# A Fourier filter and a squared-ReLU FFN in one kernel: the load of W_in, the prologue around it, and the slots of two FFT stages

## The chip, the cores and the metric

The kernel runs on one core of a Trainium2 chip. A core has five engines that work side by side and wait for each other through semaphores: PE (TensorE, matrix products into PSUM), DVE (VectorE), ACT (ScalarE), POOL (GpSimd) and SP (SyncE, which here only issues transfers). Transfers between the chip's main memory and on-chip memory run on 16 DMA engines. The metric is the device time of one execution in microseconds (us), and the median of several runs is compared.

## What is computed

x has 8 batches of 3008 positions and 256 channels. Each batch is filtered along its positions in the frequency domain, and every filtered position then goes through a feed-forward network (FFN) with 2048 hidden units:

```python
X = np.fft.rfft(x, axis=1)
Y = X * (filt_r + 1j * filt_i)[None, :, :]
y = np.fft.irfft(Y, n=3008, axis=1)            # (8, 3008, 256)
h = np.maximum(y.reshape(24064, 256) @ w_in, 0.0)
out = h * h @ w_out                            # (24064, 256)
```

Inputs and output are float32; the products on PE are made in float16 with float32 sums.

## The kernel before

**FFT stages.** 3008 = 64 x 47, so both transforms are matrix products in two steps. Of one batch: stage A multiplies x with a 47-point matrix (result u), u goes through main memory (dU) and comes back in another order as ut; stage B multiplies ut with a 64-point matrix, and DVE multiplies the result with the filter (unit_b: one product of 128 x 1024 values, two copies; unit_s: an addition); stage P is the way back (ze), which goes through main memory (dZ) and returns as zt; stage Y gives y, stored as yt. A batch has 16 units of A, 12 of B and P, 16 of Y.

**FFN.** The 24064 rows are cut into 47 groups of 512. A group takes eight slots. In each slot `ffn_g1` makes four 512-column matmuls with W_in for this group, ACT applies ReLU to the 128 x 1024 result, DVE squares it (`ffn_sq`), and `ffn_g2` makes eight 256-column matmuls with W_out for the group before. The first group (slots 0 to 7) has no group before it.

**Order.** Nothing is reordered: each engine works through its instructions in program order. The loop at L731 emits a slot at a time, and `fft_plan(b)` says into which slot, and at which of two places in it, each FFT unit of batch b goes (`put(slot, place, unit)`). Slots are counted from 40 to 48 before the group in which batch b begins; for batch 1 they are the absolute slots. A unit put into a slot stands on PE between that slot's matmuls, on DVE and ACT between the squares and ReLUs, and its transfers stand in SP's queue.

**Prologue.** All of batch 0's stages up to the first quarter of Y, and three quarters of stage A of batch 1, are made ahead of the FFN loop (L653 to L723). There stage A of batch 0 is `chunk_a0` (its result is turned by `turn_u`); `place_f(im, k)` spreads the filter's real (im = 0) or imaginary part over sF with PE, copied out by an engine that is given; `unit_p0` is stage P; `chunk_a` is stage A of batch 1. x of batches 0 and 1 comes by `load_wide` in three tiles of 1 MB, cast to float16 by `cast_wide`. Before `unit_b` of batch 0 starts, `place_f` has run for (0,0) to (0,3) and (1,0).

**Buffers.** A pool hands out its buffers in turn, and a new tile waits until all readers of the buffer's last tile are done. p_x32 has two buffers of 8 KB per partition: in turn x of batch 0 (two tiles), W_in (two tiles of 1 MB), x of batch 1 (two tiles). p_u has three: two of sSPx (a second copy of stage P's weights, made by POOL), then u of batch 1, chunks 0, 2, 1, 3 in that order. p_y has two: filt_r and filt_i, x of batch 1 (third tile), the products of batch 0, then yt. PSUM is split among psF, psO and psH, two buffers each; all FFT units in the FFN loop use psF.

**Queues.** SP issues nearly all transfers in program order. In the prologue: x of batch 0 (the first two tiles in halves), the filters, constants, W_in, the third tile of x of batch 1; then the writes of dZ, between which the other two tiles of x of batch 1 stand (L709); then two reads of zt, half of W_out, two reads of zt, the other half, and three writes of dU.

Of the kernel before, what the change touches and what calls it, by code (L numbers as in the profile page):

```python
# [9 lines left out]
F16 = mybir.dt.float16  # L10
F32 = mybir.dt.float32
# [7 lines left out]
N1, N2, NC, NM = 64, 47, 24, 32  # L19
# [91 lines left out]
def kernel(  # L111
# [96 lines left out]
    sPF = p_out.tile([128, 6, 128], F16, tag="ost", name="sPF")  # L208

    xw32, xw16 = {}, {}  # L210
    halves, later = ((0, 0), (0, 1)), []

    def load_wide(b, k):

        v0 = xrows[b * S:b * S + 2048, :].rearrange("(p m) d -> p m d", m=16)
        v1 = xrows[b * S + 2048:b * S + 3072, :].rearrange("(p m) d -> p m d", m=8)
        pool, tag = (p_x32, "x32") if k < 2 else (p_y, "yt") if b else (p_h2, "h2")
        t = pool.tile([128, 8, D], F32, tag=tag, name=f"xw_{b}_{k}")
        v = (v0[:, 0:8, :], v1, v0[:, 8:16, :])[k]
        for m in (slice(0, 4), slice(4, 8)) if (b, k) in halves else (slice(0, 8),):  # L220
            if m.stop > 4 and m.start == 4:
                later.append((t, v, m))
            else:
                nc.sync.dma_start(out=t[:, m, :], in_=v[:, m, :])
        xw32[(b, k)] = t

    def cast_wide(b, k, *engs, parts=(0, 1)):
        if 0 in parts:
            xw16[(b, k)] = p_x16.tile([128, 8, D], F16, tag="x16", name=f"xw16_{b}_{k}")
        for i in parts:  # L230
            m = slice(4 * i, 4 * i + 4)
            engs[i].tensor_copy(out=xw16[(b, k)][:, m, :], in_=xw32[(b, k)][:, m, :])

    for k in range(2):
        load_wide(0, k)
    for t, v, m in later:
        nc.sync.dma_start(out=t[:, m, :], in_=v[:, m, :])
    load_wide(0, 2)


    f32s = []
# [33 lines left out]

    f16s = []

    def place_f(im, k, eng, rotate=False):

        if rotate:  # L280
            banks, groups = bank_pair(f"psf_{im}_{k}")
        else:
            t = psH(f"psf_{im}_{k}")
            banks, groups = [t[:, 0, :], t[:, 1, :]], [(t, 0)]
        for i in range(4):
            c = 4 * k + i
            e0, e1 = D * c, D * (47 - c)
            cuts = [0] + [d for d in range(1, D)
                          if (e0 + d) % QF == 0 or (c and (e1 + d) % QF == 0)] + [D]
            for d0, d1 in zip(cuts, cuts[1:]):  # L290
                o = banks[i // 2][:, (i % 2) * D + d0:(i % 2) * D + d1]
                q, a = divmod(e0 + d0, QF)
                nc.tensor.matmul(o, sPF[:, PQ.index((0, q)), :], f16s[0][:, im, a:a + d1 - d0],  # L293
                                 start=True, stop=False)
                q, a = divmod(e1 + d0, QF) if c else (0, QF + d0)
                nc.tensor.matmul(o, sPF[:, PQ.index((1, q)), :], f16s[0][:, im, a:a + d1 - d0],  # L296
                                 start=False, stop=True)
        for t, i in groups:
            n = t.shape[1]
            dst = sF[:, im, 4 * k + 2 * i:4 * k + 2 * i + 2 * n, :]  # L300
            src = t.rearrange("p t (a d) -> p (t a) d", d=D)
            if eng is nc.scalar:
                eng.activation(out=dst, in_=src, func=AF.Copy, scale=sign[:, 0:1] if im else 1.0)  # L303
            elif im:
                eng.tensor_scalar_mul(out=dst, in0=src, scalar1=sign[:, 0:1])
            else:
                eng.tensor_copy(out=dst, in_=src)
# [2 lines left out]
    sWout = const.tile([128, NJT, 256], F16, name="sWout")  # L310
    w32s = {}

    def load_win(k):
        w32s[k] = p_x32.tile([128, DFF], F32, tag="x32", name=f"win32_{k}")
        nc.sync.dma_start(out=w32s[k], in_=moe_w_in[128 * k:128 * k + 128, :])

    def cast_win(k):
        for j in range(2):
            c = slice(1024 * j, 1024 * j + 1024)
            nc.gpsimd.tensor_copy(out=sWin[:, k, c], in_=w32s[k][:, c])  # L320

    def load_wout(k):
        if k == 0:
# [22 lines left out]
    def unit_a(b, a):  # L346

        c, i = divmod(a, 4)
        if i == 0:
            us[(b, c)] = p_u.tile([96, 8, D], F16, tag="u", name=f"u_{b}_{c}")  # L350
        ps = psF(f"psA_{b}_{a}")
        m = slice(2 * i, 2 * i + 2)
        if b == 1:
            nc.tensor.matmul(ps[0:96, :], s1[:, c // 2, :], xw16[(b, 2 * (c % 2))][:, m, :],
                             start=True, stop=False)
            nc.tensor.matmul(ps[0:96, :], s1[0:120, 2 + c, :], xw16[(b, 1)][0:120, m, :],
                             start=False, stop=True)
        else:
            nc.tensor.matmul(ps[0:96, :], sSA, x16s[(b, c)][:, m, :], start=True, stop=True)  # L359
        o = us[(b, c)][:, 2 * i:2 * i + 2, :]  # L360
        pv = ps[0:96, :].rearrange("p (a d) -> p a d", d=D)
        if a % 2 == 0:
            nc.scalar.copy(out=o, in_=pv)  # L363
        else:
            nc.vector.tensor_copy(out=o, in_=pv)  # L365
        if i == 3:
            write_u(b, c)
# [21 lines left out]
                else:  # L389
                    eng.tensor_copy(out=o, in_=pv)  # L390

    def chunk_a0(c, ks):

        for k in ks:
            banks, groups = bank_pair(f"psA_0_{c}_{k}")
            for dt in range(2):
                for i in range(4):
# [210 lines left out]
    def fft_plan(b):  # L608
# [3 lines left out]
        def put(r, place, f, *a):  # L612
            plan.setdefault((r, place), []).append((f, a))

        if b == 1:
            for n in range(4, 16):
                put(n if n < 8 else n + 2 if n < 12 else 2 * n - 7, n % 2, unit_y, 0, n)
            for k in range(4):
                put((4, 5, 7, 7)[k], 1, cast_wout, k, nc.vector)
        t0 = 2 if b == 1 else 6  # L620
        for a in range(12 if b == 1 else 0, 16):
            put(t0 + a // 2, a % 2, unit_a, b, a)
        put(10 if b == 1 else 14, 1, read_u, b)
        t0 = 14 if b == 1 else 18
        for p in range(12):
            r = t0 + (18 if b == 1 else 19) * p // 11
            put(r, 0, unit_b, b, p)
            put(r, 0, unit_s, b, p)
            put(r + 2, 1, unit_p, b, p)
        t0 = 35 if b == 1 else 40  # L630
        for c in range(4):
            put(t0, 1, read_z, b, c)
        if b + 1 < B:
# [5 lines left out]
                if c < 2:  # L639
                    put(r, 1, load_x, b + 1, c + 2)  # L640
        for n in range(16):
            if b == 1:
                put(38 + n // 2 if n > 3 else 39, n % 2, unit_y, b, n)
            else:
                put(44 + n // 2, n % 2, unit_y, b, n)
        return plan

    def run(plan, r, place):
# [2 lines left out]


    uT = p_h2.tile([128, 2, NC, 128], F16, tag="h2", name="uT")  # L653
    for i in range(2):
        for k in range(2):
            cast_wide(0, k, nc.vector, nc.vector, parts=(i,))
    cast_wide(0, 2, nc.vector, nc.gpsimd)

    def load_const(t, d, k):
        c = slice(12 * k, 12 * k + 12)  # L660
# [2 lines left out]
    for k in range(2):  # L663
        c = slice(12 * k, 12 * k + 12)
        load_const(sSB[:, c, :], dSB, k)
        load_const(sSP[:, c, :], dSP, k)
    for k in range(2):
        load_win(k)
    for k in range(2):
        for c in (0, 2):  # L670
            chunk_a0(c, (k,))
    for k in range(2):
        for c in (1, 3):
            chunk_a0(c, (k,))
    f16s.append(p_h2.tile([128, 2, QF + D], F16, tag="h2", name="f16"))
    e0, e1 = slice(0, 1504), slice(1504, QF)
    for im in range(2):
        nc.gpsimd.tensor_copy(out=f16s[0][:, im, QF:], in_=nyq[:, im, :])
    for im, e in ((0, e0), (0, e1), (1, e0)):
        nc.gpsimd.tensor_copy(out=f16s[0][:, im, e], in_=f32s[im][:, e])  # L680
    for k in range(2):
        sSPx.append(p_u.tile([128, 12, 128], F16, tag="u", name=f"sSPx_{k}"))
        c = slice(12 * k, 12 * k + 12)
        nc.gpsimd.tensor_copy(out=sSPx[k][0:64], in_=sSP[64:128, c, :])
        nc.gpsimd.tensor_copy(out=sSPx[k][64:128], in_=sSP[0:64, c, :])
    for k in range(2):
        cast_win(k)
    uts[0] = p_ut.tile([128, NC, D], F16, tag="ut", name="ut_0")
    load_wide(1, 2)
    cast_wide(1, 2, nc.gpsimd, nc.gpsimd)  # L690
    for k in range(6):
        turn_u(k, nc.vector if k in (1, 3, 4, 5) else nc.scalar)
        if k > 2:
            place_f(0, k - 3, nc.scalar, True)
    nc.vector.tensor_copy(out=f16s[0][:, 1, e1], in_=f32s[1][:, e1])
    place_f(0, 3, nc.vector, True)
    place_f(1, 0, nc.scalar)
    for k in range(7):
        if k < 6:
            unit_b(0, 2 * k)  # L700
            if k < 5:
                place_f(1, k + 1, nc.scalar)
            unit_b(0, 2 * k + 1)
        if k > 0:
            unit_p0(k - 1)
        if k < 2:
            place_f(0, k + 4, nc.scalar)
        if k in (1, 2):
            load_wide(1, k - 1)  # L709
            cast_wide(1, k - 1, nc.gpsimd, nc.gpsimd)  # L710
    read_z(0, 0)
    load_wout(0)
    read_z(0, 1)
# [59 lines left out]
```

## Time and profile before

| | |
|---|---|
| median of 7 runs | 795.35 us (794.32 to 798.26) |
| the profiled execution | 798.78 us, of which the span from the first to the last instruction is 797.0 us |
| mean clock granted to PE | 0.995 |
| first FFN matmul (psH, L560) | starts at 52.71 us |
| first W_out matmul (psO, L577; slot 8) | starts at 63.87 us |
| DMA engines | 46.6% of the span busy with SP's queue |

Times in the profile count from the start of the span. In the chain of work each line is a start, a duration, and the engine and line that ran or the transfer that was waited for. In the table of stretches the columns are: length, busy time of PE, of PE's weight loads, of DVE, ACT and POOL (with the number of instructions), granted PE clock as a share of full, busy share of the DMA engines, and GB/s. In the table of waits: who waited, for whom, us in total, number of times, the longest. In SP's timeline: start, us, line, and what is issued, with the number of transfers in a merged row.

### The profile page before, as it was taken

What the parts mean: (1) busy time and instruction counts of PE and PEld (TensorE: products, weight loads), DVE (VectorE), ACT (ScalarE), POOL (GpSimd) and SP (SyncE); (2) the same over time, 40 slices, a digit from 0 to 9 for tenths busy, and PEclk for the clock granted to TensorE, in tenths of its full rate; (3) what the DMA queues carried; (4) which work ended last, traced back from release to release, by engine and by line L of the source; (5) the groups of instructions that cost most, each with busy time, mean ns of one, the idle gap of its engine ahead of it and who ended that gap; (6) DMA issues with size and microseconds to landing.
All of it is one profiled execution on the core that took longest, in us unless ns stands there. A gap on an engine that the chain in (4) does not pass through costs nothing.

```text
span 797.0 us, 14801 instructions
## 1 busy us (share of the span) xinstructions
PE 783.5 (98%) x6102; PEld 553.7 (69%) x6102; DVE 552.3 (69%) x898; ACT 554.9 (70%) x708; POOL 24.7 (3%) x27
## 2 busy tenths in 40 slices
PE   8989999999999999999999999999999999999998
PEld 5846677667676677867778676776767666776666
DVE  6946995579755897559965699557995579554342
ACT  3856777767767677767776677676777767766664
POOL 3710000000000000000000000000000000000000
PEclk9989999999999999999999999999999999999999
DMA  9994555336713468055471555425564342521111
GB/s 353 358 274 138 136 144 140 91 127 166 207 52 107 151 163 188 29 162 152 125 183 49 169 156 134 131 68 158 149 176 95 87 138 80 122 52 41 40 41 53
DMA packets 88139, 107.32 MB, mean 135 GB/s; under 512 B 6288, under 2 KB 78864, under 8 KB 83856
## 3 DMA queue, kind: packets, MB, share of 16 engines
q1 hardware_dynamic: 87864, 106.19, 46.6%
q8 instruction: 48, 0.79, 0.4%
q10 hardware_dynamic: 144, 0.18, 0.1%
q14 instruction: 19, 0.16, 0.1%
q0 software_dynamic: 64, 0.00, 0.0%
HBM read 58.12 MB, written 48.23 MB: 133 GB/s over the span
## 4 chain that ended last, share of the span: by engine, by line
PE 92%; DMA 4%; ACT 1%; DVE 1%; issue 0%; POOL 0%; SPq 0%; ACTq 0%; DVEq 0%; POOLq 0%
PE psO L577 40%; PE psH L560 38%; PE psA L359 3%; PE psY L530 3%; PE psB L443 2%; PE psP L494 2%; DMA ut<-dU 2%; PE warm L274 1%; DMA xw<-in_x_dram 1%; PE psf L293 1%; DMA zt<-dZ 1%; ACT h L564 1%; PE psf L296 1%; DMA dU<-u 0%; PE psA L380 0%; ACT sF L303 0%
## 5 line engine op out<-in xcount | busy, mean ns | idle before, releaser
L564 ACT ACTIVATE h<-psH 128x1024 f16<-128x1024 f32 x376 | 385.2, 1025 | 190.7 <-PE psH L560 189.2
L577 PE MATMUL psO<-sWout,h 128*128 128x256 f16 x3008 | 388.6, 272 | 0.0
L560 PE MATMUL psH<-yt,sWin 128*128 128x512 f16 (+7 forms) x1728 | 386.9, 351 | 1.8 <-DVE yt L539 0.8
L577 PEld LDWEIGHTS <-h 128*128 128x128 f16 x3008 | 290.5, 98 | 77.3
L568 DVE TENSOR_TENSOR h<-h 128x1024 f16<-128x1024 f16 x376 | 253.8, 685 | 100.7 <-ACT h L564 99.2
L560 PEld LDWEIGHTS <-sWin 128*128 128x128 f16 x1728 | 159.5, 98 | 101.7 <-issue 3.5
L451 DVE TENSOR_TENSOR prod<-psB,sF 128x1024 f16<-128x1024 f32 x84 | 102.4, 1219 | 6.9 <-PE psB L443 6.6
L539 DVE CAST yt<-psY 128x376 f16<-128x376 f32 x62 | 33.9, 549 | 57.4 <-PE psY L530 57.4
L365 DVE CAST u<-psA 96x512 f16<-96x512 f32 x50 | 34.3, 687 | 47.3 <-PE psA L359 45.1
L496 ACT CAST ze<-psP 128x512 f16<-128x512 f32 x84 | 49.3, 586 | 17.8 <-PE psP L494 15.9
L588 ACT COPY ost<-psO 128x512 f32<-128x512 f32 (+1 forms) x96 | 55.7, 580 | 6.7 <-PE psO L577 5.3
L530 PEld LDWEIGHTS <-zt 112*128 112x128 f16 x512 | 34.8, 98 | 12.2 <-issue 2.4
L530 PE MATMUL psY<-sC,zt 112*128 112x94 f16 x512 | 42.3, 205 | 0.6 <-DMA zt<-dZ 0.3
L465 DVE TENSOR_TENSOR yf<-prod,yf 128x512 f16<-128x512 f16 x84 | 35.7, 425 | 2.9
L443 PE MATMUL psB<-ut,sSB 128*128 128x256 f16 x192 | 36.5, 272 | 1.2 <-DMA ut<-dU 0.9
L359 PE MATMUL psA<-x,sC 94*96 94x512 f16 x96 | 36.6, 382 | 0.0
L443 PEld LDWEIGHTS <-sSB 128*128 128x128 f16 x192 | 18.6, 98 | 21.9 <-issue 2.8
L494 PE MATMUL psP<-yf,sSP 128*128 128x256 f16 x168 | 32.1, 273 | 0.2 <-ACT yt L537 0.2
L537 ACT CAST yt<-psY 128x376 f16<-128x376 f32 x66 | 30.7, 468 | 1.1 <-PE psY L530 0.6
L338 DVE CAST x<-x 94x2048 f16<-94x2048 f32 x24 | 29.2, 1216 | 0.0
L363 ACT CAST u<-psA 96x512 f16<-96x512 f32 x50 | 28.6, 572 | 0.0
L458 DVE COPY yf<-prod 64x512 f16<-64x512 f16 x84 | 24.3, 289 | 2.9
(63 smaller groups left out, 256.5 us busy)
## 6 DMA issues: line engine op xcount, KB each, us to landing
x<-in_x_dram SPq DMA_DIRECT2D x20, 768.0 KB
zt<-dZ SPq DMA_DIRECT2D x64, 192.0 KB
dU<-u SPq DMA_DIRECT2D x28, 384.0 KB
dZ<-ze SPq DMA_DIRECT2D x28, 384.0 KB
out_dram<-ost SPq DMA_DIRECT2D x66, 128.0 KB
out_dram<-ost SPq DMA_DIRECT2D x31, 256.0 KB
ut<-dU SPq DMA_DIRECT2D x7, 1024.0 KB
xw<-in_x_dram SPq DMA_DIRECT2D x4, 1024.0 KB
```

The source lines that it names most:

```text
L359: nc.tensor.matmul(ps[0:96, :], sSA, x16s[(b, c)][:, m, :], start=True, stop=True)
L443: nc.tensor.matmul(ps[:, i * D:(i + 1) * D], sSB[:, 2 * p + i, :], uts[b][:, 2 * p + i, :], start=True, stop=True)
L451: nc.vector.tensor_mul(out=prod, in0=ps.rearrange("p (a d) -> p a d", d=D).unsqueeze(1).to_broadcast([128, 2, 2, D]), in1=sF[:, :, 2 * p:2 ...
L465: nc.vector.tensor_add(out=yf, in0=prod[:, 0], in1=yf)
L494: nc.tensor.matmul(ps[:, i * D:(i + 1) * D], sSP[:, 2 * p + i, :], yf[:, i, :], start=True, stop=True)
L496: nc.scalar.copy(out=zes[(b, c)][:, 2 * i6:2 * i6 + 2, :], in_=ps.rearrange("p (a d) -> p a d", d=D))
L530: nc.tensor.matmul(ps[:, 94 * jj:94 * jj + 94], zt[:, 4 * (g % 2) + jj, dt * 128:(dt + 1) * 128], sSY, start=True, stop=True)
L560: nc.tensor.matmul(ps[:, i, o:o + n], sWin[:, dt, jt * 128:(jt + 1) * 128], yts[b][:, dt, r:r + n], start=(dt == 0), stop=(dt == 1))
L564: nc.scalar.activation(out=h2[:, 2 * s:2 * s + 2, :], in_=ps, func=AF.Relu)
L568: nc.vector.tensor_mul(out=v, in0=v, in1=v)
L577: nc.tensor.matmul(pso[g][:, t % 2, :], h2s[g][:, jt, t * 128:(t + 1) * 128], sWout[:, jt, :], start=(jt == 0), stop=(jt == NJT - 1))
L588: nc.scalar.copy(out=ost[:, h0:h0 + step, :], in_=pso[g][:, h0:h0 + step, :])
```

## The change

- W_in is loaded in seven pieces of 256 to 768 columns, into buffers of p_ze, p_prod and p_yf that nobody uses yet. All three x tiles of batch 1 are therefore issued right after it, ahead of the writes of dZ. POOL casts the seven pieces.
- x of batch 0 is loaded in whole tiles, and `chunk_a0` goes chunk by chunk.
- In `turn_u`/`place_f`: only (0,0), (0,1) and (1,0) come before `unit_b` of batch 0; (0,2) to (0,5) come between its units, copied by ACT. The cast of filt_i is split over DVE, POOL and ACT. sSPx is made in six pairs of copies instead of two.
- The third x tile of batch 1 is cast by DVE and ACT after `unit_b` and `unit_p0` of batch 0; POOL casts the first two.
- Last quarter of stage A of batch 1: slots 1 to 4 instead of 8 and 9, all four copied by DVE. The Y units 8 to 11 of batch 0 sit in slots 8 to 11 instead of 10 to 13. W_out is cast by POOL in slots 1, 2, 4 and 5, instead of DVE in slots 4, 5, 7 and 7.
- Batch 1: stage B ends one slot earlier (slot 31), the reads of zt, loads and casts of x come one slot earlier, and Y takes two units in each of slots 38 to 45; before, four were in slot 39.
- Batches 2 to 7: stage B starts at offset 19 instead of 18, with the last unit at 37 as before, and Y at 45 instead of 44.

```diff
-    def load_win(k):
-        w32s[k] = p_x32.tile([128, DFF], F32, tag="x32", name=f"win32_{k}")
-        nc.sync.dma_start(out=w32s[k], in_=moe_w_in[128 * k:128 * k + 128, :])
+    def load_win():
+        for k, c, n, pool, tag in ((0, 0, 768, p_ze, "ze"), (0, 768, 768, p_ze, "ze"),
+                                   (0, 1536, 512, p_prod, "prod"), (1, 0, 768, p_ze, "ze"),
+                                   (1, 768, 512, p_prod, "prod"), (1, 1280, 512, p_prod, "prod"),
+                                   (1, 1792, 256, p_yf, "yf")):
+            t = pool.tile([128, n], F32, tag=tag, name=f"win32_{k}_{c}")
+            nc.sync.dma_start(out=t, in_=moe_w_in[128 * k:128 * k + 128, c:c + n])
+            wins.append((t, k, slice(c, c + n)))
...
-        if a % 2 == 0:
+        if a % 2 == 0 and b > 1:
             nc.scalar.copy(out=o, in_=pv)
...
-                put(n if n < 8 else n + 2 if n < 12 else 2 * n - 7, n % 2, unit_y, 0, n)
+                put(n if n < 12 else 2 * n - 7, n % 2, unit_y, 0, n)
             for k in range(4):
-                put((4, 5, 7, 7)[k], 1, cast_wout, k, nc.vector)
-        t0 = 2 if b == 1 else 6
+                put((1, 2, 4, 5)[k], 1, cast_wout, k, nc.gpsimd)
+        t0 = 6
         for a in range(12 if b == 1 else 0, 16):
-            put(t0 + a // 2, a % 2, unit_a, b, a)
+            put(a - 11 if b == 1 else t0 + a // 2, a % 2, unit_a, b, a)
         put(10 if b == 1 else 14, 1, read_u, b)
-        t0 = 14 if b == 1 else 18
+        t0 = 14 if b == 1 else 19
         for p in range(12):
-            r = t0 + (18 if b == 1 else 19) * p // 11
+            r = t0 + (17 if b == 1 else 18) * p // 11
...
-        t0 = 35 if b == 1 else 40
+        t0 = 34 if b == 1 else 40
...
-            if b == 1:
-                put(38 + n // 2 if n > 3 else 39, n % 2, unit_y, b, n)
-            else:
-                put(44 + n // 2, n % 2, unit_y, b, n)
+            put((38 if b == 1 else 45) + n // 2, n % 2, unit_y, b, n)
...
-    for k in range(2):
-        load_win(k)
-    for k in range(2):
-        for c in (0, 2):
-            chunk_a0(c, (k,))
-    for k in range(2):
-        for c in (1, 3):
-            chunk_a0(c, (k,))
+    load_win()
+    for k in range(3):
+        load_wide(1, k)
+    for c in (0, 2, 1, 3):
+        chunk_a0(c)
...
-    for im, e in ((0, e0), (0, e1), (1, e0)):
-        nc.gpsimd.tensor_copy(out=f16s[0][:, im, e], in_=f32s[im][:, e])
+    for e in (e0, e1):
+        nc.gpsimd.tensor_copy(out=f16s[0][:, 0, e], in_=f32s[0][:, e])
+    uts[0] = p_ut.tile([128, NC, D], F16, tag="ut", name="ut_0")
+    turn_u(0, nc.scalar)
+    turn_u(1, nc.vector)
+    turn_u(2, nc.scalar)
+    turn_u(3, nc.vector)
+    place_f(0, 0, nc.scalar, rotate=True)
+    for eng, e in ((nc.vector, slice(0, 1024)), (nc.gpsimd, slice(1024, 2048)),
+                   (nc.scalar, slice(2048, QF))):
+        cast(eng, f16s[0][:, 1, e], f32s[1][:, e])
+    turn_u(4, nc.vector)
+    place_f(0, 1, nc.scalar, rotate=True)
+    turn_u(5, nc.vector)
+    place_f(1, 0, nc.scalar, nc.vector, rotate=True)
...
-    for k in range(2):
-        cast_win(k)
-    uts[0] = p_ut.tile([128, NC, D], F16, tag="ut", name="ut_0")
-    load_wide(1, 2)
-    cast_wide(1, 2, nc.gpsimd, nc.gpsimd)
-    for k in range(6):
-        turn_u(k, nc.vector if k in (1, 3, 4, 5) else nc.scalar)
-        if k > 2:
-            place_f(0, k - 3, nc.scalar, True)
-    nc.vector.tensor_copy(out=f16s[0][:, 1, e1], in_=f32s[1][:, e1])
-    place_f(0, 3, nc.vector, True)
-    place_f(1, 0, nc.scalar)
+    cast_win()
+    for k in range(2):
+        cast_wide(1, k, nc.gpsimd, nc.gpsimd)
...
-        if k < 2:
-            place_f(0, k + 4, nc.scalar)
-        if k in (1, 2):
-            load_wide(1, k - 1)
-            cast_wide(1, k - 1, nc.gpsimd, nc.gpsimd)
+        if k < 4:
+            place_f(0, k + 2, nc.scalar)
+    cast_wide(1, 2, nc.vector, nc.scalar)
```

More of the change, by code (lines that the diff above doesn't have):

```diff
@@ L210 @@
     xw32, xw16 = {}, {}
-    halves, later = ((0, 0), (0, 1)), []
     def load_wide(b, k):
@@ L218, in load_wide, with cast, cast_wide @@
         t = pool.tile([128, 8, D], F32, tag=tag, name=f"xw_{b}_{k}")
[L219 to L222, printed above, removed]
-            else:
-                nc.sync.dma_start(out=t[:, m, :], in_=v[:, m, :])
-        xw32[(b, k)] = t
[L227 to L230, printed above, removed]
+        nc.sync.dma_start(out=t, in_=(v0[:, 0:8, :], v1, v0[:, 8:16, :])[k])
+        xw32[(b, k)] = t
+    def cast(eng, out, in_):
+        (eng.copy if eng is nc.scalar else eng.tensor_copy)(out=out, in_=in_)
+    def cast_wide(b, k, *engs):
+        t = p_x16.tile([128, 8, D], F16, tag="x16", name=f"xw16_{b}_{k}")
+        for i in range(2):
             m = slice(4 * i, 4 * i + 4)
-            engs[i].tensor_copy(out=xw16[(b, k)][:, m, :], in_=xw32[(b, k)][:, m, :])
-    for k in range(2):
+            cast(engs[i], t[:, m, :], xw32[(b, k)][:, m, :])
+        xw16[(b, k)] = t
+    for k in range(3):
         load_wide(0, k)
-    for t, v, m in later:
-        nc.sync.dma_start(out=t[:, m, :], in_=v[:, m, :])
-    load_wide(0, 2)
     f32s = []
@@ L276, with place_f @@
     f16s = []
-    def place_f(im, k, eng, rotate=False):
+    def place_f(im, k, *engs, rotate=False):
         if rotate:
@@ L299, in place_f @@
             n = t.shape[1]
+            eng = engs[i % len(engs)]
             dst = sF[:, im, 4 * k + 2 * i:4 * k + 2 * i + 2 * n, :]
@@ L311, with cast_win @@
     w32s = {}
-    def load_win(k):
-        w32s[k] = p_x32.tile([128, DFF], F32, tag="x32", name=f"win32_{k}")
-        nc.sync.dma_start(out=w32s[k], in_=moe_w_in[128 * k:128 * k + 128, :])
[L317 to L320, printed above, removed]
+    def load_win():
[6 more added lines that the diff above has]
+            wins.append((t, k, slice(c, c + n)))
+    def cast_win():
+        for t, k, c in wins:
+            nc.gpsimd.tensor_copy(out=sWin[:, k, c], in_=t)
+    wins = []
     def load_wout(k):
@@ L390, in chunk_a, with chunk_a0 @@
                     eng.tensor_copy(out=o, in_=pv)
-    def chunk_a0(c, ks):
-        for k in ks:
+    def chunk_a0(c):
+        for k in range(2):
             banks, groups = bank_pair(f"psA_0_{c}_{k}")
@@ L641, in fft_plan @@
         for n in range(16):
-            if b == 1:
-                put(38 + n // 2 if n > 3 else 39, n % 2, unit_y, b, n)
-            else:
-                put(44 + n // 2, n % 2, unit_y, b, n)
+            put((38 if b == 1 else 45) + n // 2, n % 2, unit_y, b, n)
         return plan
@@ L653 @@
     uT = p_h2.tile([128, 2, NC, 128], F16, tag="h2", name="uT")
-    for i in range(2):
-        for k in range(2):
-            cast_wide(0, k, nc.vector, nc.vector, parts=(i,))
-    cast_wide(0, 2, nc.vector, nc.gpsimd)
+    for k in range(3):
+        cast_wide(0, k, nc.vector, nc.gpsimd if k == 2 else nc.vector)
     def load_const(t, d, k):
@@ L666 @@
         load_const(sSP[:, c, :], dSP, k)
-    for k in range(2):
-        load_win(k)
-    for k in range(2):
-        for c in (0, 2):
-            chunk_a0(c, (k,))
-    for k in range(2):
-        for c in (1, 3):
-            chunk_a0(c, (k,))
+    load_win()
+    for k in range(3):
+        load_wide(1, k)
+    for c in (0, 2, 1, 3):
+        chunk_a0(c)
     f16s.append(p_h2.tile([128, 2, QF + D], F16, tag="h2", name="f16"))
@@ L678 @@
         nc.gpsimd.tensor_copy(out=f16s[0][:, im, QF:], in_=nyq[:, im, :])
-    for im, e in ((0, e0), (0, e1), (1, e0)):
-        nc.gpsimd.tensor_copy(out=f16s[0][:, im, e], in_=f32s[im][:, e])
-    for k in range(2):
[L682 to L686, printed above, removed]
-        cast_win(k)
-    uts[0] = p_ut.tile([128, NC, D], F16, tag="ut", name="ut_0")
-    load_wide(1, 2)
-    cast_wide(1, 2, nc.gpsimd, nc.gpsimd)
-    for k in range(6):
-        turn_u(k, nc.vector if k in (1, 3, 4, 5) else nc.scalar)
-        if k > 2:
-            place_f(0, k - 3, nc.scalar, True)
-    nc.vector.tensor_copy(out=f16s[0][:, 1, e1], in_=f32s[1][:, e1])
-    place_f(0, 3, nc.vector, True)
-    place_f(1, 0, nc.scalar)
+    for e in (e0, e1):
[13 more added lines that the diff above has]
+    place_f(1, 0, nc.scalar, nc.vector, rotate=True)
+    for k in range(6):
+        if k % 3 == 0:
+            sSPx.append(p_u.tile([128, 12, 128], F16, tag="u", name=f"sSPx_{k}"))
+        c, o = slice(4 * k, 4 * k + 4), slice(4 * k % 12, 4 * k % 12 + 4)
+        nc.gpsimd.tensor_copy(out=sSPx[-1][0:64, o, :], in_=sSP[64:128, c, :])
+        nc.gpsimd.tensor_copy(out=sSPx[-1][64:128, o, :], in_=sSP[0:64, c, :])
+    cast_win()
+    for k in range(2):
+        cast_wide(1, k, nc.gpsimd, nc.gpsimd)
     for k in range(7):
```

## The prediction

> **What bounds the kernel now.** I read the page first: engines, then the chain that ended last, then the chain's first 90 us piece by piece, the table of stretches, and last PE's waits after 90 us.
>
> ```profile
> PE 783.5 (98%) x6102; PEld 553.7 (69%) x6102; DVE 552.3 (69%) x898; ACT 554.9 (70%) x708; POOL 24.7 (3%) x27
> ...
> PE 92%; DMA 4%; ACT 1%; DVE 1%; issue 0%; POOL 0%; SPq 0%; ACTq 0%; DVEq 0%; POOLq 0%
> ```
>
> PE sets the end, and the change adds and removes no matmul. So its worth is PE time that is not at full pace: idle, or at half clock. I took each matmul's distance to the next, less the usual distance of its shape. The excess is 13.8 us before 80 us, of which 5.8 before 40 (2.5 of it the warm-up), and 6.9 us in all the rest. The chain shows the early part:
>
> ```profile
> 33.06 1.00 ACT ze L482
> 34.08 0.38 SPq L483
> 34.56 7.14 DMA xw<-in_x_dram
> 41.74 0.08 issue
> 41.83 1.05 POOL xw L232
> 42.92 0.59 PE psA L380
> ...
> 52.71 0.38 PE psH L560
> ```
>
> Stage A of batch 1 waits for the last third of its x, whose load stood behind a dZ write in SP's queue and waited for the W_in buffers. What follows the wait is slow as well:
>
> ```profile
> 40.00:45.00 5.00, 2.89 (x10) 1.47 (x10) 0.28 (x1) 2.18 (x3) 2.03 (x2) 0.71 0.80 247
> 45.00:50.00 5.00, 5.00 (x16) 2.47 (x15) 2.00 (x3) 1.21 (x2) 0.00 (x0) 0.61 0.83 234
> ```
>
> The seventh number is the clock (0.71, 0.61): from 42.9 to 48.9 us the 512-column matmuls start 0.427 us apart, then 0.216. After 90 us:
>
> ```profile
> PE psB L443 <- DMA ut<-dU: 0.9, 2, 0.8
> PE psH L560 <- DVE yt L539: 0.3, 1, 0.3
> PE psY L530 <- DMA zt<-dZ: 0.3, 1, 0.3
> PE psY L530 <- ACT yt L537: 0.3, 1, 0.3
> ```
>
> By the matmul distances[...] psB lost 0.33, 0.93, 0.16, 0.28 and 0.30 us (at 166, 262, 453, 548, 643), psY 0.47 and 0.13 (217, 599), and the slot with four Y units 0.43 + 0.21 + 0.47 (127 to 129).
>
> [...]half clock for 6.8 us, after a stretch in which PE stood idle for 0.42, 0.52 and 1.77 us within 4.3. [...]POOL's 1024-column cast took 1.56 us beside a DVE cast, 1.04 alone.[...]
>
> **Main loop, step by step.** Moving B of batches 2 to 7 one slot later gives each ut load some 2 us more (a slot is 1.74 to 2.18 us). All five waits are under 1 us: 2.00 us gone. Y one slot later: 0.60 gone. Four Y units spread over slots 38 and 39: of 1.11 us some 0.3 stays, since slot 40 still needs the last copy (0.55 us on DVE) at once: 0.8 gone. Together 3.4.
> What it costs: the twelve B units, about 2.15 us of DVE each, are squeezed into 18 slots where there were 19, between casts of x (1.22 us) in slots 32 and 35. Stage P follows two slots later and waits for DVE. The smallest slack between the last add and its P matmul is 0.61 us for batch 2 now. The new offsets of units 8 to 11 (32, 33, 35, 37, casts at 32 and 35) are those of batch 1 now (27, 28, 30, 32, casts at 27 and 30), where the last slacks are 0.50, 0.98, 0.12 us and PE shows no stall. I take 0.1 us in all (bounds 0 and 2.4). Sum: -3.3 us (-1.0 to -3.6).
>
> **Prologue.** *x in whole tiles*: the same bytes land; the first A matmul needs the cast ended at 10.16 us, and the warm-up matmuls hold PE until 10.9. Nothing, as long as they do; without them 2.7 us. *filt_i cast in three*: it lands at 21.10. DVE's third ends at 21.85,[...] POOL's by 22.2 to 22.7 (1.04 to 1.56). The first place of im = 1 then ends on ACT at 24.6, and the first product starts there instead of at 26.31. But two more place copies (1.02 us each) now stand between ACT's ze copies. Ahead of the last ze copy ACT has 5 x 1.11 + 4 x 1.02 + 5 x 1.01 = 14.7 us, so not before 39.3; DVE's twelve products (1.155 us apart) are held by it, and the last ends at 39.75 (now 40.28). Last ze copy: 40.3 to 41.3 (now 40.97 to 41.98). Of 1.7 us, 0.7 is left. (The pair of engines given to this place changes nothing: its banks come as one group, so ACT alone copies.)
> *W_in in seven pieces, x of batch 1 early*: SP's issue waits for the landing of the issue eight before it (issues at 6.67, 8.23, 9.47, 11.96, 15.66, 21.16; landings at 6.66, 8.21, 9.45, 11.94, 15.58, 21.10). So the pieces go out from 15.6 to 24.4 and the three x tiles from 25.3 to 27.2, ahead of every dZ. From 25.24 us on 5.24 MB at 1.05 MB per 2.5 us land by 37.8. POOL, 12 sSPx copies, 4.1 us of W_in and four x casts (1.04), ends at 38.5; the last tile is cast by DVE and ACT by 42.4. A of batch 1 needs the first at 40.3, the last at 44.7. Wait and half clock go: A ends at 45.5, not 51.06.
> *What is late next*: Y needs the second zt read, issued when the last dZ landed. Now 41.98, 44.85, issue 44.87, landed 48.02. With a ze copy 0.7 us earlier[...]: issue 43.6, landed 46.8. PE idles 1.3 us; W_in's first group starts 1.85 us after that (as 50.86 to 52.71): at 48.7, 4.0 us earlier.
> *Last quarter of A in slots 1 to 4*: four pairs, 0.43 us of PE each, leave slots 8 and 9. But u of chunk 3 takes the buffer of u of chunk 0 (p_u has 3; two hold sSPx), so DVE's first copy waits until that write to dU has landed. SP issues it behind two zt reads and 2.1 MB of W_out:
>
> ```profile
> 45.28 0.39 SPq L326 DMA_DIRECT2D wout<-in_moe_w_out_dram  x1
> 45.72 1.03 SPq L512 DMA_DIRECT2D zt<-dZ  x2
> 46.79 0.65 SPq L326 DMA_DIRECT2D wout<-in_moe_w_out_dram  x1
> 47.54 7.33 SPq L342 DMA_DIRECT2D dU<-u  x3
> ```
>
> It landed at 57.79, 12.9 after the zt issue; so now at 56.5. Before, the copy came at 65.4 and never waited. Behind it on DVE stand the squares and Y's copies; on PE, psF has two banks, so the third pair, in slot 3, waits for the first copy, until 57.25. PE has by then done slots 0 to 3 (by about 52.5) and idles 4.8 us[...]. What remains of the group then is four slots of W_in, two A pairs and four Y units: 4 x 0.87 + 2 x 0.43 + 4 x 0.17 = 5.0 us at full clock.[...] Slot 8 at 64.8; slots 8 and 9 at 1.92 each; slot 10 at 68.65, now 67.79. Y units that left slots 12 and 13 give 0.35 back: **+0.5 us** (-0.4 to +1.4).
> *cast_wout on POOL* (four of 1.04): W_out lands at 50.1 and 54.9, done by 57, first needed in slot 8. Nothing; it frees DVE of 2.7 us, and four A copies there add 1.4.
>
> **Sum**: -3.3 + 0.5 = -2.8 us. The profiled execution took 798.78 (span 797.0), 3.4 above the median; the difference carries over: 795.35 - 2.8 = **792.5 us**.
>
> **Rivals.** *Full clock after the wait*: [...]the 2.55 us go: prologue -2.0, total 790.0. Against: one idle of 1.77 us was enough before. *No wait on dU*: if the write lands early, or the buffer is another, PE goes on until slot 8, where Y needs zt_2, landed 61.7 before, so 60.4: slot 10 at 63.4, total -8.1: 787.2. Against: three buffers, and W_out in front. *DVE becomes the bound in stage B*: 0.4 us more delay in each of six batches eats 2.4 us: 794.9. For: slack 0.12. Against: batch 1. *The write to dU lands late (slower)*: slot 10 comes 12.1 us after its landing, so each us later costs one, and from 60.9 on the sum passes +1.6. [...]in the profile one dU issue took 2.84 us. At 62.5: 798.6.
>
> **Chances.** Likeliest 0.58 (its own range 791 to 794), full clock 0.22, no wait 0.07, DVE 0.05, late dU 0.08. A measurement of this kernel tells about 0.2%, 1.6 us. Faster: 0.52 + 0.22 + 0.07 + 0.01 = 0.82; same: 0.06 + 0.04 = 0.10; slower 0.08. The range runs from the no-wait case to the DVE case, 787.2 to 795.0, and leaves out the late write and half a tail.
>
> **What would show it.** Right: no DMA wait before L380; the first slot of W_in near 48.7; a DVE copy of u near 56.5 released by DMA dU<-u, PE idle 4 to 5 us before the third pair, a clock below 1 from there to about 62; no psB or psY wait on DMA after 90 us. Wrong: if A of batch 1 still waits for its x, if the copy of u starts by 52, or if psP waits for DVE at the end of each B stage.

## The result, and the profile after

The changed kernel takes 798.69 us in the median of 12 runs (797.82 to 800.25); the kernel before, measured beside it and earlier, 795.99 us in the median of 31 (793.94 to 798.65). The ratio is 1.0034, with a 95% interval of 1.0023 to 1.0046: 2.7 us slower (1.8 to 3.7). Forecast was 2.8 us faster, 792.5 us.

The two profiled executions do not show this: 796.8 us of span after, 797.0 before. The page after, first engines, then the chain's shares:

```profile
PE 780.7 (98%) x6102; PEld 553.0 (69%) x6102; DVE 550.1 (69%) x895; ACT 556.7 (70%) x709; POOL 28.1 (4%) x40
...
PE 92%; DVE 4%; DMA 2%; ACT 1%; SPq 0%; issue 0%; ACTq 0%; DVEq 0%
```

PE is busy as before and on the chain as before. DMA's share fell from 4% to 2%, DVE's rose from 1% to 4%. Of the waits of PE after 80 us none is on a transfer any more, and what is left is mostly DVE's (the shortest waits are not listed):

```profile
PE psO L579 <- DVE h L570: 0.6, 1, 0.6
PE psP L496 <- DVE prod L453: 0.3, 1, 0.3
PE psP L496 <- ACT yt L539: 0.2, 1, 0.2
PE psH L562 <- DVE yt L541: 0.2, 1, 0.2
```

The early part of the chain after (start, duration, what) has the wait that was forecast:

```profile
41.08 1.02 ACT ze L484
42.11 2.37 DMA dZ<-ze
...
47.12 10.47 DMA dU<-u
57.61 0.05 DVEq L367
57.71 0.70 DVE u L367
58.45 0.38 PE psA L356
```

The write of u to dU, issued at 47.12 behind W_out, landed at 57.6; then DVE copied the first u of the moved quarter, and the third A pair could start. The stretches (length; busy time of PE, weight loads, DVE, ACT, POOL; clock; DMA share; GB/s) show what that costs:

```profile
50.00:55.00 5.00, 3.97 (x19) 1.78 (x17) 1.51 (x1) 3.95 (x4) 2.48 (x2) 1.00 1.07 271
55.00:60.00 5.00, 1.55 (x5) 0.66 (x5) 2.29 (x4) 0.03 (x1) 2.02 (x2) 0.87 1.12 351
60.00:65.00 5.00, 5.00 (x29) 2.43 (x28) 3.83 (x7) 3.29 (x4) 0.00 (x0) 0.78 0.48 116
```

PE stands idle for 4.5 us, ACT for 5.9, and from 58.75 to 62.16 us the clock is half. All this is in the forecast. What was not: another profiled execution of the kernel before, with a span of 793.9 us (called the full-clock execution from here on), has no half clock in stage A of batch 1. The same two stretches that the prediction shows, in that execution, and its longest wait from 40 to 80 us:

```profile
40.00:45.00 5.00, 3.13 (x16) 1.74 (x15) 1.06 (x2) 2.08 (x3) 2.03 (x2) 1.00 0.81 246
45.00:50.00 5.00, 4.63 (x39) 2.88 (x38) 3.80 (x6) 3.02 (x5) 0.00 (x0) 1.00 0.93 252
...
PE psA L380 <- POOL xw L232: 1.9, 1, 1.9
```

The clock is 1.00 where the first profile had 0.71 and 0.61, although PE waits for x as long (1.87 us; 1.77 in the first profile). The start of some FFN slots, from the matmul records, in us:

| slot | before, first profile | before, full-clock execution | after |
|---|---|---|---|
| 0 | 52.71 | 49.52 | 49.31 |
| 8 | 61.92 | 58.72 | 65.56 |
| 10 | 67.79 | 64.59 | 69.97 |
| 34 | 116.23 | 113.04 | 119.50 |
| 42 | 132.82 | 129.62 | 135.16 |
| 375 (last group's last) | 784.71 | 781.65 | 784.41 |

Against the full-clock execution the change starts the FFN 0.2 us earlier, loses 7.0 us in the first group (16.25 instead of 9.20), gains 1.5 in slots 8 and 9 (the quarter has left them), loses 0.2 up to slot 42 and gains 2.8 from there to the end: 2.8 us later at the last slot, close to the measured difference of the medians.

### The profile page after: what moved, and what is told of

Its sections match the earlier page's. It is cut to its first block, busy times and chain, and to the rows that moved or that the text cites. A ratio compares the mean times of both kernels' runs of the same rounds, so it can differ in the third digit from the quotient of the medians.

```text
span 796.8 us, 14814 instructions
## 1 busy us (share of the span) xinstructions
PE 780.7 (98%) x6102; PEld 553.0 (69%) x6102; DVE 550.1 (69%) x895; ACT 556.7 (70%) x709; POOL 28.1 (4%) x40
## 4 chain that ended last, share of the span: by engine, by line
PE 92%; DVE 4%; DMA 2%; ACT 1%; SPq 0%; issue 0%; ACTq 0%; DVEq 0%
PE psO L579 40%; PE psH L562 39%; PE psA L361 3%; PE psY L532 3%; PE psB L445 2%; PE psP L496 2%; DMA dU<-u 1%; DVE prod L453 1%; PE warm L268 1%; DVE h L570 1%; PE psf L287 1%; PE psf L290 1%; ACT sF L298 0%; ACT h L566 0%; DVE yf L467 0%; DVE prods L453 0%
## 5 line engine op out<-in xcount | busy, mean ns | idle before, releaser
L566 ACT ACTIVATE h<-psH 128x1024 f16<-128x1024 f32 x376 | 385.0, 1024 | 195.1 <-PE psH L562 192.9
```

The source lines that it names most:

```text
L566: nc.scalar.activation(out=h2[:, 2 * s:2 * s + 2, :], in_=ps, func=AF.Relu)
```

## The experiments

Each is compared with the kernel before on the same chip; ratios can be compared between the runs, medians less so, since the kernel before took 796.0 to 797.0 us on the chips used. Where a loss at a matmul is given to a hundredth, it is its distance to the next, less the usual distance, as in the prediction; the view of waits gives up to 0.2 us less.

**The kernel before, again** (no edit).

> The kernel before, unchanged, to see how its executions spread. Theory 1 (the profiled execution of before held a spell of half clock that most executions do not have): the spans fall into a low group near 792 to 794 us at a granted clock of 0.997 to 0.999 and a high one near 796 to 797 at about 0.995; a median execution has no half-clock matmul in stage A of batch 1, or a shorter spell. Rival (every execution has the spell, and the profiled one was long for another reason): the clock is 0.995 in nearly all, whatever the span, and a profile shows the spell at 42 us again.

795.99 us, ratio 0.9995 (0.9983 to 1.0008). Each execution lists its span and mean clock. The 61 executions of the kernel before beside this run and three of those below fall into groups:

| mean clock | executions | spans, us |
|---|---|---|
| 0.995 to 0.996 | 9 | 796.3 to 797.9 |
| 0.997 to 0.998 | 31 | 794.6 to 796.7 |
| 0.999 to 1.000 | 21 | 792.6 to 794.8 |

The traces of the kernel before and after hold 6.83 us (mean 0.995) and 3.41 us (0.997) at half clock, the last 0.8 us of the span aside. 3.41 us lower a mean of 797 us by 0.002, so the groups are taken, as an estimate from these numbers, to have 6.83 us of it, 3.41, and none; no trace shows an execution of the middle group, and where its half clock lies is not shown. The first profile (0.995) is of the rarest group. The rival, that nearly all have the spell in full, falls; the theory was too strong as well, since by this estimate half of these executions have 3.41 us of it. The shares vary: of all 137 executions of the unchanged kernel beside these runs and in this one, 17, 61 and 59 fall into the three groups. The profiled execution of this run was again of the first group (0.995).

**The kernel before, one more execution** (no edit).

> The kernel before once more, one look. If this execution has full clock from the warm-up on, its first FFN matmul starts near 49.2 to 49.8, not 52.7, and its span is 793 to 794; if it has the spell, as in the first profile, 52 to 53 and 796 to 798.

Mean clock 1.000, span 793.9, first FFN matmul at 49.52: the full-clock execution quoted above.

**Before, PE kept busy in the wait.**

```diff
+    psw = psO("warm2").rearrange("p a d -> p (a d)")
+    for _ in range(8):
+        nc.tensor.matmul(psw, zero, sF[:, 0, 0:2, :], start=True, stop=True)
     for c in (0, 2, 1):
         chunk_a(1, c)
```

> The kernel before with eight 512-column matmuls on zeros (1.7 us at full clock) ahead of stage A of batch 1, in the time in which PE waits for its x. Theory 1: no execution has the half clock after the wait, the spread shrinks at its upper end, and the median stays within 0.7 us of before (794.5 to 796.2). Rival (the half clock is in every execution of before): it goes, and the median falls by 2 to 3 us.

796.97 us, ratio 1.0000 (0.9991 to 1.0008); mean clock 0.999 or 1.000 in all 21 executions, spans 793.2 to 796.1. So with these matmuls the clock stays full, and the median stays, as the theory has it. But the spans are not as short as the full-clock ones of before (median 795.1 against 793.6 us), so the unchanged median does not by itself show that the half clock costs the median nothing. In its trace slot 0 starts at 49.69 and slot 80 at 206.38, 0.3 us behind the full-clock execution, and then 1.57 us are lost at 214 us, where Y waits for zt. Why that wait is longer here than in other traces with these slots (0.44 to 0.85) stays open.

**The quarter of A moved back.** The Y units 8 to 11 go back with it, and ACT takes half of the copies again.

```diff
-        if a % 2 == 0 and b > 1:
+        if a % 2 == 0:
...
-                put(n if n < 12 else 2 * n - 7, n % 2, unit_y, 0, n)
+                put(n if n < 8 else n + 2 if n < 12 else 2 * n - 7, n % 2, unit_y, 0, n)
...
-            put(a - 11 if b == 1 else t0 + a // 2, a % 2, unit_a, b, a)
+            put(2 + a // 2 if b == 1 else t0 + a // 2, a % 2, unit_a, b, a)
```

> The changed kernel with the last quarter of stage A of batch 1 back in slots 8 and 9 (units and engines as before, Y units 8 to 11 back in slots 10 to 13). Theory: the wait for the write of dU is what makes the change slower; without it PE does not idle at 54 to 58 us nor fall to half clock, slot 8 starts at 59 to 60 instead of 65.6, A's four pairs cost 1.7 us again: 4 to 5 us faster than the changed kernel, 794 to 795, or 1 to 2 us below before. Rival (what the wait hid is late anyway: W_out or zt for the next slots): less than 1.5 us faster than the changed kernel.

794.27 us, ratio 0.9974 (0.9966 to 0.9983): 0.6% below the changed kernel, so the quarter, with its Y units and copies, costs some 4.8 us. Slot 8 starts at 60.26. This is the main loss.

**The quarter alone, on the kernel before.** The copies of u (all on DVE), the Y units 8 to 11 and the casts of W_out (on POOL) go with it; their lines are left out here.

```diff
...
-        t0 = 2 if b == 1 else 6
+        t0 = 6
...
-            put(t0 + a // 2, a % 2, unit_a, b, a)
+            put(a - 11 if b == 1 else t0 + a // 2, a % 2, unit_a, b, a)
```

> The kernel before with one part of the change alone: the last quarter of A in slots 1 to 4, its Y units in slots 8 to 11, W_out cast by POOL. Theory: the write of dU lands at about 57.7 as before, so the third pair starts near 58.5 whether PE ran at half clock before or not; slot 10 comes near 68 to 69, where an execution of before at full clock has it near 65 and one with the half-clock spell at 68: slower than before by 1 to 3 us (797 to 799.5), and the spread of the executions shrinks. Rival (the quarter alone does no harm; the wait arises only with the earlier start of the FFN): within 0.7 us of before.

799.84 us, ratio 1.0055 (1.0040 to 1.0070): 4.4 us slower, more than expected. In its trace the FFN starts at 49.15, so PE reaches the third pair early and waits:

```profile
PE psA L354 <- DVE u L365: 4.2, 1, 4.2
```

Slot 10 starts at 69.27, 4.7 after the full-clock execution. The rival, that the quarter harms only beside the new prologue, falls.

**u in another buffer.** Nothing is moved; the tile of chunk 3 comes from p_x16.

```diff
-            us[(b, c)] = p_u.tile([96, 8, D], F16, tag="u", name=f"u_{b}_{c}")
+            pool, tag = (p_x16, "x16") if b == 1 else (p_u, "u")
+            us[(b, c)] = pool.tile([96, 8, D], F16, tag=tag, name=f"u_{b}_{c}")
```

> The changed kernel, but u of chunk 3 of batch 1 takes a buffer of p_x16, which is long free, instead of the one of chunk 0: everything stays where the change put it, only what the copy of u waits for is gone. Theory (that wait is the loss): no wait for dU, PE goes on to slot 8, where Y may wait some 1.5 us for zt_2 (it landed at 60.7 and 61.5); slot 10 at 64 to 65 instead of 70.1: 5 us faster than the changed kernel, 793 to 794, and 0.5 to 1.5 below the run with the quarter moved back. Rival (DVE with four copies of u more, or ACT, limits the first group anyway): not faster than the run with the quarter moved back.

793.8 us, ratio 0.9973 (0.9961 to 0.9985): as fast as with the quarter moved back, and 0.6% below the changed kernel. Slot 8 starts at 60.56 instead of 65.56. With everything else in the same slots this shows the wait for the buffer to be the cause. The waits of PE from 40 to 80 us in this run:

```profile
PE psY L533 <- DMA zt<-dZ: 1.3, 1, 1.3
PE psA L357 <- DVE u L368: 0.9, 1, 0.9
PE psH L563 <- DVE yt L542: 0.6, 1, 0.6
PE psP L483 <- DVE prods L454: 0.5, 1, 0.5
PE psH L563 <- ACT yt L540: 0.5, 2, 0.3
PE psY L531 <- ACT u L391: 0.3, 1, 0.3
```

The wait for u is 0.9 us, not 4.5, and it is for DVE's pace. The expected 0.5 to 1.5 us below the run with the quarter moved back are not there within the intervals, so the rival's number came true: slot 10 is 1.3 us earlier in its trace, but the other trace has half clock at 50 us (a granted clock of 0.66 from 50 to 55), and the medians do not resolve it.

**The write of u ahead of W_out.**

```diff
     read_z(0, 0)
-    load_wout(0)
-    read_z(0, 1)
-    load_wout(1)
     for c in (0, 2, 1):
         chunk_a(1, c)
-    for c in (0, 2, 1):
+        if c == 0:
+            write_u(1, 0)
+            load_wout(0)
+            read_z(0, 1)
+            load_wout(1)
+    for c in (2, 1):
         write_u(1, c)
```

> The changed kernel with the write of chunk 0's u to dU issued right after the reads of the first zt tile, ahead of W_out and of the second zt tile; no buffer is changed. Theory (the wait is as long as the queue in front of that write): it lands at 48 to 49 instead of 57.6, the copy of u in slot 1 does not wait, and the kernel is 4 to 5 us faster than the changed one (0.3% below before), as with u in another buffer. Rival (W_out and zt, each 1 us later, are then waited for): 2 us or less.

795.54 us, ratio 0.9988 (0.9980 to 0.9996): 3.7 us faster than the changed kernel, between theory and rival. The write lands at 48.9 and nothing waits for it; but what it overtook is later, and is waited for:

```profile
PE psY L532 <- DMA zt<-dZ: 3.4, 3, 1.2
PE psH L562 <- DVE yt L541: 0.9, 1, 0.9
```

Two of the three zt waits (losses of 1.33 and 1.25 us, at 54.9 and 62.3 us) are new. Slot 10 starts at 66.69, 1.6 us behind the run with u in another buffer. The DMA engines' busy share is over 1 from 50 to 60 us here and still 0.77 from 60 to 65: the transfer that went ahead moved others back.

**The changed kernel, PE kept busy in the wait.**

```diff
+        if (b, a) == (1, 14):
+            psw = psO("warm3").rearrange("p a d -> p (a d)")
+            for _ in range(20):
+                nc.tensor.matmul(psw, zero, sF[:, 0, 0:2, :], start=True, stop=True)
         if b == 1:
```

> The changed kernel with 20 matmuls on zeros (512 columns, 4.3 us) in slot 3 ahead of the third A pair, in the time in which PE waits for the write of dU. Theory (the idle costs twice: the wait, and half clock behind it): the wait stays, the clock stays full, and the median falls by 1.0 to 1.8 us, the excess that the trace of the changed kernel shows from 58.5 to 62. Rival (behind the wait DVE limits, with its squares and copies late, so the half clock is hidden): within 0.5 us of the changed kernel.

798.1 us, ratio 1.0031 (1.0018 to 1.0043), not told apart from the change. The clock is full:

```profile
55.00:60.00 5.00, 4.95 (x23) 2.20 (x22) 2.07 (x4) 0.36 (x1) 2.02 (x2) 1.00 1.14 354
60.00:65.00 5.00, 4.13 (x31) 2.24 (x30) 4.40 (x9) 3.61 (x5) 0.00 (x0) 1.00 0.62 160
```

and slot 8 starts at 65.24, against 65.56. DVE works with no gap over 0.1 us from 57.9 to 63.6, on four copies of u, the squares that had waited behind the first one, and Y's copy: at full clock it limits the group. At half clock, in the trace of the changed kernel, it has one gap, 0.73 us of waiting for the fourth pair. The rival holds: the half clock is nearly hidden. From the third pair to slot 8 it takes 7.11 us with it and 6.57 without.

**Stages B and Y of batches 2 to 7 alone, on the kernel before.**

```diff
-        t0 = 14 if b == 1 else 18
+        t0 = 14 if b == 1 else 19
...
-            r = t0 + (18 if b == 1 else 19) * p // 11
+            r = t0 + (18 if b == 1 else 18) * p // 11
...
-                put(44 + n // 2, n % 2, unit_y, b, n)
+                put(45 + n // 2, n % 2, unit_y, b, n)
```

> The kernel before with one part of the change alone: stages B and Y of batches 2 to 7 one slot later. From the two traces, PE's excess after 160 us fell from 5.1 to 2.8 us: 2 to 2.5 us faster than before (793.5 to 794.0). If stage B's tighter slots cost DVE time that shows only elsewhere: less than 1 us.

794.53 us, ratio 0.9976 (0.9967 to 0.9985): 1.9 us faster (1.2 to 2.6), as the theory has it. In the trace of the changed kernel the slack between the last three adds and their P matmuls in batch 2 is 0.50, 0.99 and 0.13 us, the pattern that batch 1 had before, and PE does not stall on it.

**The new prologue alone.** The changed kernel with the whole `fft_plan` of before, and ACT for half of the copies of u; W_out is cast by DVE again. Some of the lines:

```diff
...
-                put(n if n < 12 else 2 * n - 7, n % 2, unit_y, 0, n)
+                put(n if n < 8 else n + 2 if n < 12 else 2 * n - 7, n % 2, unit_y, 0, n)
...
-            put(a - 11 if b == 1 else t0 + a // 2, a % 2, unit_a, b, a)
+            put(t0 + a // 2, a % 2, unit_a, b, a)
...
-            put((38 if b == 1 else 45) + n // 2, n % 2, unit_y, b, n)
+            if b == 1:
+                put(38 + n // 2 if n > 3 else 39, n % 2, unit_y, b, n)
+            else:
+                put(44 + n // 2, n % 2, unit_y, b, n)
```

> The changed prologue (W_in in pieces, x of batch 1 early, the order of the places and casts) with the slots of before for everything in the FFN loop. Theory 1 (what it removes, the wait for x, costs most executions of before little, since Y then waits for zt, and the spell of half clock is in some of them only): first FFN matmul near 49.4, within 0.15% of before, and a narrower spread. Rival (the prologue is worth the 3 to 4 us that the two traces show at the first FFN matmul): 3 us faster than before, 0.4%.

796.82 us, ratio 1.0003 (0.9991 to 1.0014): no change in the median. Slot 0 starts at 50.00, and Y has the wait in x's place:

```profile
PE psY L532 <- DMA zt<-dZ: 1.4, 1, 1.4
```

The spread is narrower, as expected. Fewer executions have half clock (6 of 14 by the mean clock, 21 of 35 of the kernel before beside it), but the full-clock ones have a span of 794.7 us in the median, before 793.75; why these are longer is not shown.

The parts add up: quarter +0.55%, B and Y of batches 2 to 7 -0.24%, prologue +0.03%, together +0.34%, the measured ratio. The slots of batch 1 were not run alone; by this sum they are left with about nothing, within some 0.2% that the intervals leave.

**Towards a faster version.** u in p_x16; Y units 8 to 11 and, for batch 1, the B units and casts of x in the slots of before:

```diff
...
-                put(n if n < 12 else 2 * n - 7, n % 2, unit_y, 0, n)
+                put(n if n < 8 else n + 2 if n < 12 else 2 * n - 7, n % 2, unit_y, 0, n)
...
-            r = t0 + (17 if b == 1 else 18) * p // 11
+            r = t0 + 18 * p // 11
...
             put(t0, 1, read_z, b, c)
+        if b == 1:
+            t0 = 35
```

> The changed kernel with u of chunk 3 in p_x16, Y units 8 to 11 of batch 0 in slots 10 to 13 as before, and for batch 1 the B units and the casts of x in the slots of before (reads of zt at 34, two Y units per slot stay). Theory: it avoids the waits that the trace of the changed kernel still shows (zt_2 in slot 8; the adds and squares late at 98 and 118 us, 1.2 us together): 1 to 2 us faster than the run with u elsewhere alone, 791.5 to 793. Rival (the Y units or the squares wait at another slot): the same as that run within 0.5 us.

793.56 us, ratio 0.9967 (0.9956 to 0.9978): faster than both kernels; not told apart from the run with u elsewhere alone (0.9973), so the expected 1 to 2 us are not there. Its trace lost 1.0 us to zt of batch 1 at 120 us. So, with batch 1's B from slot 13 to 30:

```diff
-        t0 = 14 if b == 1 else 19
+        t0 = 13 if b == 1 else 19
...
-            r = t0 + 18 * p // 11
+            r = t0 + (17 if b == 1 else 18) * p // 11
```

> The fastest version so far (u in p_x16, Y units 8 to 11 and the casts of batch 1 as before), with the B units of batch 1 from slot 13 on, the last in slot 30, so that its zt is written two slots earlier. Its trace lost 1.0 us to that zt at 120 us: 0.5 to 1 us faster than that version, 0.40 to 0.45% below before. If ut is not there by slot 13, or the squares of slot 31 come late, the same or slower.

794.02 us, ratio 0.9968 (0.9955 to 0.9980): no gain. The zt wait is still 0.92 us, and a P matmul waits 0.91 us at 85.5.

## Why the prediction was wrong

**The step that failed: "the difference carries over".** The sum was made against a profiled execution 3.4 us above the median of its runs, and this surplus was taken for something that every execution shares. It had a place: the half clock from 42.1 to 48.9 us, quoted in the prediction itself. By the mean clocks, most executions have 3.41 us of it or none. The prediction counted its removal as gain ("Wait and half clock go", FFN 4.0 us earlier), and then started from a median in which it was mostly absent. Against the full-clock execution the FFN starts 0.2 us earlier, not 4.0, and the new prologue alone changes the median by nothing that could be measured.

This step is 3.4 of the 6.2 us by which the forecast was off. Without it the sum gives 798.78 - 2.8 = 796.0 us, no change against the 795.99 measured with it. The other 2.7 us are terms of the sum itself: 1.3 up to slot 10 and 1.3 between slots 10 and 42, both below. Nearly all signs named under "What would show it" came true (first slot at 49.31, idle of 4.5 us, half clock to 62.16, no psB or psY wait on a transfer after 90 us): they tell of the mechanism in one trace and could not show that the starting point was wrong.

**Why the wait for x was worth nothing.** Y needs the second zt read, which landed at 47.73 after and at 47.91 in the full-clock execution, where PE had just ended stage A (its first Y matmul on zt is at 48.05). The prediction named it as late next, but put it at 46.8, since it expected the last ze copy 0.7 us earlier, from a sum of copies without gaps. After, that copy starts at 41.08 (40.97 before). It waits for DVE's last product, which ends at 40.40 (forecast 39.75): DVE stood idle twice, for 0.96 and 0.98 us, which the profile puts down to ze copies on ACT, and ahead of most of ACT's copies some 0.1 us is lost, ahead of the last but one 0.3. The cast of filt_i was not what held it: ACT's third took 0.98 us, and the first product starts at 24.43 (forecast 24.6).

**The wait for dU was right**, in place and order: landing 57.59 (forecast 56.5), third pair 58.45 (57.25), idle 4.5 us (4.8). Slot 10 came at 69.97 (68.65), 1.3 us late: 1.2 of it come with the landing. From the third pair to slot 8 it took 7.11 us, where the forecast had 5.0 of work and 2.55 more for the half clock. The 2.55 was the author's assumption, which no trace shows; that the sum is near is luck. The run with the clock held took 6.57, so the half clock costs 0.5 us, not 2.55, and the rest of the group takes 1.5 us more than the 5.0 of PE's own time, since DVE's late copies and squares limit it. Waits for Y's copies in slot 8 (0.45 us for DVE's, 0.20 for ACT's) then make slots 8 and 9 take 4.41 us, where the forecast had 3.84. At slot 10 the changed kernel is 2.2 us behind the execution with the spell, which the prediction (+0.9 there) compared with, and 5.4 behind the one without.

**Main loop**: for batches 2 to 7 it was -2.5; measured -1.9 (-1.2 to -2.6) alone, -2.8 from slot 42 on between the two traces. This part was right. For batch 1 it was -0.8, and -0.35 for Y units that left slots 12 and 13; but from slot 10 to 42 the change takes 65.19 us, before 65.03. The four Y units lost less (0.35 us instead of 1.1). But g2 in slot 33 loses 0.76 us to squares that stand behind the last B unit, which now ends one slot ahead of a group boundary, and a P matmul loses 0.44 at 98 us. The prediction had looked at the slack of stage P alone, not at the squares.

**The rivals**: the slower one (a dU landing from 60.9 us on) had the right transfer, but its threshold came from the same wrong starting point: 3.2 us earlier at slot 10, it is 57.7, and the write landed at 57.59.

## What to carry to other kernels

When the profiled execution lies off the median, find the stretch that makes it so before summing anything; here half clock came with a wait of 1.77 us in one trace and not with one of 1.87 in another, and one profile showed one of three cases. Before an early wait is removed, take the time of the next thing that the stage waits for: if it comes at the same moment, the wait is worth nothing. A unit that is moved to an earlier slot needs its buffer earlier, and so waits for the buffer's last reader; where that reader is a transfer behind others in a queue (here a write that landed 10.47 us after its issue), the queue sets the slot.

## What the runs showed of the hardware

In the trace before, the granted clock falls to half at 42.10 us and is full again 6.83 us later; in the trace after it falls at 58.75 and is full again 3.41 us later. Before the fall it had been full for 34.13 and 51.20 us; in these two traces all four lengths are whole multiples of 3.41 us (2, 1, 10, 15). The fall of before came in a wait for x of 1.77 us. In the full-clock execution the clock was 1.00 from 40 to 50 us with such a wait of 1.87 us, so the length of the wait does not decide it. The 3.41 us that ended at the fall held 1.89 us of idle PE in the trace before and 3.11 in the trace after. What decides is not shown.

DVE's square of 128 x 1024 values takes 0.69 us (changed kernel, from 64 us on). Where it began 0.05 to 0.12 us after a cast of W_out on POOL it took 1.51 us (changed kernel), 1.53 and 1.45 (u in another buffer). Three others that ran in part or wholly beside such casts, with the quarter moved back, took 1.00, 0.79 and 1.15 us; one that began 0.46 us ahead of the cast, in the same trace, took 0.69. The copy of a PSUM tile at 53.22 us in the run with u in another buffer, wholly beside a cast, took 0.67, as without one (0.68).
